# Folding the feature map into the projection weights: phi as the moving side, in two halves of the array

## The chip, the cores and the metric

The kernel runs on one core of a Trainium2 chip. The metric is the device time of one execution in microseconds (us), the median of the runs. A core has five engines that run side by side, each through its own list of instructions in order: TensorE (PE, with its weight loads shown apart as PEld), VectorE (DVE), ScalarE (ACT), GpSimd (POOL) and SyncE (SP), which here issues almost every DMA.

## The reference, cut to what matters

Two linear-attention blocks A and B of the same shape work on the same input and are mixed by a gate. Shapes: 2048 tokens, width 448, 16 heads of 28.

```
qkv   = x @ wqkv                      # per block: q, k, v, each 2048 x 448
pq,pk = q @ w_phi, k @ w_phi          # per head, 28 x 28
phi   = concat(softmax(p), softmax(-p))
kv    = phi_k^T v ;  z = sum phi_k    # per head
o     = phi_q kv / (phi_q z + 1e-6)
out   = g * (o_A @ wo_A) + (1 - g) * (o_B @ wo_B),   g = sigmoid(x . gate_w)
```

Softmax doesn't change when a constant is taken from all 28 features of a head. So phi may be folded into the weights, `x @ (wqkv_k @ w_phi)`, and the 28th feature subtracted from the others: 27 columns per head are left, 432 per block.

## The kernel before, in words

**Precision and tiles.** Every large product runs in fp32r (an fp32 of fewer mantissa bits) with both operands split into a high and a low part. A projection of one tile of 128 tokens for one block is 11 matmuls into one PSUM bank: 4 chunks of 128 rows high by high, 4 high by low, 3 low by high. The 2048 tokens are 16 tiles; two tiles share one load of x (512 KB, 256 tokens), called x0, x1, x2 and so on below. Each load is split by ACT (high) and DVE or POOL (low) into `rx`.

**Stages.** First the weights: `wv` (values, with the gate's column) is loaded and split; `wkt` and `wqt` (keys and queries, transposed, 448 rows of 512 columns per block) are loaded raw, multiplied by phi on the PE (the **fold**, four of them: K and Q for blocks A and B) and split into `rk` and `rq`. Then for each tile: values (V: banks `VA` and `VB`, one per block), keys (K: bank `K`), queries (Q: bank `Q`), softmax parts on ACT, DVE and POOL, and `kv_acc`, which adds phi_k by v into `T0`. At the end, from about 246 us, numerator, division, gate and output product.

**The fold before** (`load_wp`, `load_wt`, `fold`). The raw weights of one block stand in four groups of 28 partitions (one head each at partition 0, 32, 64, 96), loaded by four DMAs of 224 KB. The stationary side is `wpd`, phi less its 28th column, 28 x 32; the moving side is 128 columns of raw weights. That is 64 matmuls in fp32 per fold, on 16 tiles of 32 x 32 of the array, into a tensor `F` of four PSUM banks. The result has features in partitions, so DVE transposes all of `F` in one instruction (128 x 2048) into `ft` in SBUF; after that, four times, ACT copies a chunk to the high part and DVE (for two chunks of each Q fold POOL) subtracts to get the low part. `F` is one key: the next fold's matmuls wait until the transpose has read all of it.

**What sets the order.** All work is entered into a `Plan` by `add(engine, cost, ..., reads, writes)` in the order of `steps()`. PE keeps that order (`order` chains the PE steps). For the other engines and for SP a list scheduler picks, by the costs written in the code, the ready step with the earliest due time; SP steps also go through a model of the DMA queue, `moved = max(moved, t + 0.8) + kb / 360`, with the `kb` given to `add`. The list that comes out is fixed: on the chip every engine takes its instructions in that order and waits where one isn't ready. In `load_wt` the `kb` entered was 460 for a DMA of 224 KB. SP keeps eight DMAs in flight: a ninth waits for the first to land.

**Buffers.** `wkt` lies in `rt` slots 1 and 2. `wqt` lies in `re`, where the raw `wv` lay before, so it waits until `wv` is split. `ft` lies in `rt` slot 0 and in `ru`.

## Time and profile before

| What | Value |
|---|---|
| runs | 349.86, 349.91, 350.72 us; median 349.91 |
| profiled execution | 348.77 us, span of its instructions 347.0 us |
| granted TensorE clock | 0.998 of full |
| PE busy | 331.9 us (96% of the span) |
| DVE, POOL, ACT busy | 282.9 us (82%), 241.0 (69%), 145.8 (42%) |
| first key projection starts | 44.41 us |
| first query projection starts | 55.54 us in the chain of waits |
| numerator stage starts | 245.8 us |

The page's slices give each engine's busy share over time; the chain of waits follows the work that ended last back to its start; the table of windows gives busy time per stage, with the rate at which DMAs moved data. A matmul in fp32 leaves two records of a weight load and two of a matmul, so 64 matmuls are "x128".

### The profile page before, as it was taken

Reading aid. Unit: us, or ns where it says so; the run is one execution under the profiler, and the core shown is the slowest. Engines: PE = TensorE matmul, PEld = TensorE weight load, DVE = VectorE, ACT = ScalarE, POOL = GpSimd, SP = SyncE. Lnnn points to the kernel's source line nnn. Section 1 sums busy time; section 2 is a strip of 40 time slices with the busy share of each in tenths; the row PEclk is TensorE's granted clock in tenths of the full one; section 3 lists DMA queues with packets and bytes.
Section 4 is the critical chain, followed back from the end, with each engine's and each line's share of the span. In section 5 each row is a group of like instructions: output and inputs, shape, how many; then the busy total and the mean of one; then the engine's idle time right before and its main releaser. Section 6 shows DMA issues by size and latency. Waiting matters only on the chain.

```text
span 347.0 us, 9268 instructions
## 1 busy us (share of the span) xinstructions
PE 331.9 (96%) x3976; PEld 297.9 (86%) x3976; DVE 282.9 (82%) x342; ACT 145.8 (42%) x219; POOL 241.0 (69%) x195
## 2 busy tenths in 40 slices
PE   6985999999999999999999999999999999999995
PEld 5764799999999999999999999999888887787895
DVE  3647687897988979879898899987599999989780
ACT  3525684446426436345344543243043333443231
POOL 3003077999999988996987987795087769777600
PEclk9999999999999999999999999999999999999999
DMA  7998620641267497366536323377875545231111
GB/s 247 219 203 185 184 74 3 202 135 44 58 243 255 140 291 254 117 201 264 158 64 288 108 55 105 90 238 267 281 256 176 188 176 204 64 138 42 43 53 53
DMA packets 29488, 55.21 MB, mean 159 GB/s; under 512 B 4304, under 2 KB 23248, under 8 KB 27144
## 3 DMA queue, kind: packets, MB, share of 16 engines
q1 hardware_dynamic: 29320, 54.52, 50.1%
q8 instruction: 31, 0.51, 0.6%
q0 software_dynamic: 128, 0.12, 0.1%
q14 instruction: 9, 0.07, 0.1%
HBM read 32.00 MB, written 24.22 MB: 162 GB/s over the span
## 4 chain that ended last, share of the span: by engine, by line
PE 70%; DVE 16%; DMA 5%; POOL 3%; ACT 2%; issue 2%; SPq 1%; POOLq 0%; DVEq 0%; ACTq 0%
PE K L380 20%; PE Q L380 19%; PE VA L380 9%; PE VB L380 8%; PE O L597 8%; DVE rv L560 4%; PE T L467 4%; DMA re<-in_xt 3%; POOL rt L266 2%; DMA re<-in_wv 2%; DVE rt L512 2%; DVE T L585 2%; PE N L549 2%; DVE qsm L507 1%; DVE rx L266 1%
## 5 line engine op out<-in xcount | busy, mean ns | idle before, releaser
L380 PE MATMUL K<-rk,rx 128*128 128x432 f32 x352 | 72.2, 360 | 0.0
L380 PE MATMUL Q<-rq,rx 128*128 128x432 f32 x352 | 72.0, 359 | 0.0
L597 PE MATMUL O<-rk,rx 128*128 128x448 f32 x336 | 70.4, 368 | 1.5 <-ACT rx L269 1.5
L597 PEld LDWEIGHTS O<-rk,rx 128*128 128x128 f32 x336 | 62.5, 188 | 9.8 <-ACT rx L269 3.0
L380 PEld LDWEIGHTS Q<-rq,rx 128*128 128x128 f32 x352 | 66.0, 188 | 3.5 <-DVE ru L266 0.4
L380 PEld LDWEIGHTS K<-rk,rx 128*128 128x128 f32 x352 | 65.8, 188 | 3.5 <-issue 0.2
L266 POOL TENSOR_TENSOR re<-re,sm 128x896 f32<-128x896 f32 x32 | 54.0, 1709 | 6.2 <-DVE sm L456 5.2
L269 ACT ACTIVATE re<-re 128x896 f32<-128x896 f32 x32 | 30.5, 953 | 31.7 <-POOL re L266 31.7
L266 POOL TENSOR_TENSOR rt<-qmn,ru 128x896 f32<-128x896 f32 x16 | 28.3, 1766 | 16.9 <-DVE rt L512 10.9
L380 PE MATMUL VA<-rv,rx 128*128 128x450 f32 x154 | 34.7, 371 | 5.3 <-issue 3.6
L455 DVE TENSOR_REDUCE sm<-re 128x32 f32<-128x896 f32 x32 | 33.8, 1072 | 4.4 <-ACT re L269 4.4
L507 DVE TENSOR_REDUCE qsm<-rt 128x32 f32<-128x896 f32 x32 | 34.0, 1067 | 3.7 <-ACT rt L269 3.6
L380 PEld LDWEIGHTS VA<-rv,rx 128*128 128x128 f32 x154 | 28.5, 189 | 8.6 <-issue 4.0
L380 PE MATMUL VB<-rv,rx 128*128 128x448 f32 x154 | 33.5, 365 | 0.0
L269 ACT ACTIVATE rt<-ru 128x896 f32<-128x896 f32 x16 | 15.2, 953 | 40.3 <-issue 11.7
L380 PEld LDWEIGHTS VB<-rv,rx 128*128 128x128 f32 x154 | 28.9, 188 | 2.3
L512 DVE STREAM_TRANSPOSE rt<-rt 128x2048 f32<-128x2048 f32 x13 | 29.6, 2277 | 0.8 <-POOL rt L266 0.8
L266 POOL TENSOR_TENSOR re<-pk,mx 128x896 f32<-128x896 f32 x16 | 28.0, 1749 | 2.5 <-DVE mx L448 2.5
L266 POOL TENSOR_TENSOR rt<-rt,qsm 128x896 f32<-128x896 f32 x16 | 27.3, 1706 | 1.0
L266 POOL TENSOR_TENSOR re<-mx,pk 128x896 f32<-128x896 f32 x16 | 27.3, 1708 | 0.0
L269 ACT ACTIVATE pk<-K 128x896 f32<-128x896 f32 x16 | 14.8, 923 | 27.9 <-PE K L380 27.9
L569 POOL TENSOR_TENSOR rv<-rv,rd 128x896 f32<-128x896 f32 x14 | 23.8, 1703 | 1.1
(94 smaller groups left out, 460.5 us busy)
## 6 DMA issues: line engine op xcount, KB each, us to landing
ed<-rt SPq DMA_DIRECT2D x8, 1024.0 KB
qd<-ru SPq DMA_DIRECT2D x64, 112.0 KB
ru<-qd SPq DMA_DIRECT2D x16, 448.0 KB
re<-ed SPq DMA_DIRECT2D x5, 1024.0 KB
xraw<-in_xt SPq DMA_DIRECT2D x7, 512.0 KB
out<-re SPq DMA_DIRECT2D x16, 224.0 KB
wod<-wst SPq DMA_DIRECT2D x14, 224.0 KB
rk<-wod SPq DMA_DIRECT2D x2, 1568.0 KB
```

The lines of the kernel that those rows point to most:

```text
L266: return lambda: ENG[eng].tensor_tensor(val(o), val(a), val(b), op)
L269: return lambda: A.activation(val(o), val(i), f, **k)
L380: nc.tensor.matmul(bank[name][:, k, lo:hi], x[:, xc, o:o + P], w[l][:, c], start=i == 0, stop=i == len(XT) - 1)
L455: put("DVE", 2 * D, lambda s=s, e3=e3: V.tensor_reduce(sm[:, s], e3, AX.X, OP.add), [ke[s]], [("sm", t % 2, s)])
L467: nc.tensor.matmul(kvp()[32 * r:32 * r + DH + 1, b, g], vs[t % NV][:, b, h // 2, h % 2], es[t % NE][:, :, hs:hs + DH], start=(t == 0 and b ...
L507: put("DVE", 2 * D, lambda s=s, e3=e3: V.tensor_reduce(qsm[:, s], e3, AX.X, OP.add), [ke[s]], [("qsm", i, s)])
L512: add("DVE", 2.25, lambda: V.transpose(eTf[slot], eq.rearrange("p s a c f -> p (s a c f)")), ke, turned(slot))
L549: nc.tensor.matmul(bank["N"][32 * g:32 * g + 32, r, 2 * b * P:2 * b * P + 2 * P], kvt[32 * r:32 * r + 32, b, s, g], eTp[slots[0] // 2][32 ...
L560: add("DVE", 0.07 + 1.08 * nt, lambda: V.transpose(ctr().rearrange("p (r n) -> p r n", r=4), bank["N"][:, :, :2 * nt * P]), ["N"], [("ctr" ...
L569: put(eng, 2 * D, lambda: ENG[eng].tensor_tensor(mid["o", n % 3].rearrange("p (c a f) -> p a c f", c=4, a=8), ctv()[:, :, i, :, :DH], rd[: ...
L585: put("DVE", 4 * P + 50, lambda: V.transpose(ps().rearrange("p k (c t) -> p k c t", c=4), o()[:, :MID]), [("o", n % 3)], [kb])
L597: nc.tensor.matmul(bank[pb][:, 0, :D], a, w, start=i == 0, stop=i == len(terms) - 1)
```

## The change

The fold is turned round. The raw weights stand in two groups of 56 partitions (two heads each, at partition 0 and 64), loaded by two DMAs of 448 KB instead of four of 224. They become the stationary side: 56 x 128. The moving side is `bd`, a block-diagonal phi of 56 x 54: 27 features by two heads, zero where row and head don't belong together, made on DVE from phi and a mask that is loaded too. A fold is 32 matmuls (fp32, two halves of the array in turn), in two steps `jj` of 16, and its result has model rows in partitions and features in columns, which is the order that the projections want. The transposes and `ft` are gone: ACT and DVE read `F` in PSUM. All low parts are DVE's; POOL has none. `F` has four keys instead of one, so each step of a fold waits only for the readers of its two banks. `rk` and `rq` change their order to `b f h`, which a projection still reads as 432 columns in a row.

The buffers move as well: `wqt` goes to `rt` slot 0 and to `ru`, and no longer waits for `wv` to be split; `wpd` and `bd` lie in `ru`; `wv`'s raw rows keep `re` until the first K step. In `steps()` K 0 now stands ahead of V 4 and of the last fold. The planner's costs are new: 2.4 per fold (`FOLD`), and `kb = 917 // NB` = 458 for a DMA of 448 KB.

```diff
-    yield from (... ("FK", 0), ("x1",), ("V", 2), ("FK", 1), ("wq", 0), ("wq", 1), ("V", 3), ("x", 2))
-    yield from (("FQ", 0), ("V", 4, 0), ("FQ", 1), ("later",), ("K", 0), ("V", 4, 1), ("K", 1), ("wo_rows",))
+    yield from (... ("FK", 0), ("x1",), ("V", 2), ("FK", 1), ("wq", 0), ("wq", 1), ("V", 3), ("x", 2), ("FQ", 0), ("K", 0), ("V", 4, 0), ("FQ", 1), ("later",), ("V", 4, 1), ("K", 1), ("wo_rows",), ...
...
     def load_wt(k, b):
-        for q in range(4):
-            o, i = wts[k][b][32 * q:32 * q + DH], {"K": wkt, "Q": wqt}[k][b].rearrange("(g q d) c -> q d g c", q=4, d=DH)[q]
-            add("SP", 0.4, dma(o, i), [], [("wt", k, b, q)], lat=2, kb=460, ...)
+        for i in range(NB):
+            o = wts[k][b][64 * i:64 * i + PG]
+            r = {"K": wkt, "Q": wqt}[k][b].rearrange("(g p) c -> p g c", p=4 * DH)[PG * i:PG * i + PG]
+            add("SP", 0.4, dma(o, r), [], [("wt", k, b, i)], lat=2, kb=917 // NB, ...)
 
-    def fold(k, b, wh, wl, key, low):
...
-                        nc.tensor.matmul(bank["F"][32 * o:32 * o + 32, q, g * P:(g + 1) * P], wpd[32 * q:32 * q + DH, b, g],
-                                         wts[k][b][32 * q:32 * q + DH, g].rearrange("p (j o i) -> p o j i", o=4, i=32)[:, o], ...)
-        add("PE", 1.95, mm, [("wpd",), *[("wt", k, b, q) for q in range(4)]], ["F"])
-        add("DVE", 2.25, lambda: V.transpose(ft[b]..., bank["F"]...), ["F"], [ftk[b]])
-        for j in range(4):
-            add("ACT", 0.75, act(h, s), [ftk[b]], [(key, "h", j, b)])
-            add(e, {"DVE": 0.85, "POOL": 1.35}[e], tt(e, l, s, h.bitcast(F32), OP.subtract), ...)
+    def fold(k, b, wh, wl, key):
+        for jj in range(2):
+            def mm(jj=jj):
+                for m in range(2):
+                    for g in range(4):
+                        for i in range(2):
+                            j = 2 * jj + m
+                            nc.tensor.matmul(bank["F"][:, 2 * i + jj, :FW].rearrange("p (m f g q) -> p m g f q", ...)[:, m, g],
+                                             wts[k][b][64 * i:64 * i + PG, g, j * P:j * P + P], bd[64 * i:64 * i + PG, b, g], ...)
+            add("PE", FOLD / 2, mm, keys, [("F", 2 * i + jj) for i in range(2)])
+        for jj in range(2):
+            for i in range(2):
+                put("ACT", D, act(h, s), [("F", 2 * i + jj)], [key_h])
+                put("DVE", D + 50, tt("DVE", l, s, h.bitcast(F32), OP.subtract), [("F", 2 * i + jj), key_h], [key_l])
```

The scheduler's list moves at three places.

SP, the loads between `wv` and the third load of x. `in_xt` is x (x1 goes to `re`, the others to `xraw`), `in_wkt` and `in_wqt` are the raw weights. Before:

```order
L272 DMA rt<-in_wkt 28x4x512 x4
L272 DMA re<-in_xt 128x4x256
L272 DMA rt<-in_wkt 28x4x512 x4
L272 DMA xraw<-in_xt 128x4x256
L272 DMA re<-in_wqt 28x4x512 x8
L272 DMA xraw<-in_xt 128x4x256
```

and with the change:

```order
L273 DMA rt<-in_wkt 56x4x512 x2
L273 DMA re<-in_xt 128x4x256
L273 DMA rt<-in_wkt 56x4x512 x2
L273 DMA rt<-in_wqt 56x4x512 x2
L273 DMA ru<-in_wqt 56x4x512
L273 DMA xraw<-in_xt 128x4x256
L273 DMA ru<-in_wqt 56x4x512
```

The load of x2 (the first to `xraw` here) stood ahead of all of `wqt`; it now stands behind three quarters of it.

ACT, around the split of x2 (`rx<-xraw`); `vs_73` is the value tile 2, `vs_74` tile 3. Before:

```order
L269 ACTIVATE rx<-re 128x4x128 x2
L269 ACTIVATE vs_73<-VA 128x16x28
L269 ACTIVATE glog<-VA 128x1
L269 ACTIVATE rk<-rt 128x4x4x27 x3
L269 ACTIVATE vs_73<-VB 128x16x28
L269 ACTIVATE rx<-xraw 128x1024
L269 ACTIVATE rk<-rt 128x4x4x27
```

and with the change:

```order
L270 ACTIVATE rk<-F 128x216x2 x4
L270 ACTIVATE vs_73<-VA 128x16x28
L270 ACTIVATE glog<-VA 128x1
L270 ACTIVATE rx<-xraw 128x1024
L270 ACTIVATE vs_73<-VB 128x16x28
L270 ACTIVATE rk<-F 128x216x2 x4
```

The split of x2 stood behind the copy that empties bank `VB` of tile 2; it now stands ahead of it, and ahead of all four copies of the second K fold.

PE, from the first fold to the second key projection (`VA`, `VB` are one tile's values, `F` a fold). Before:

```order
L334 MATMUL F<-rt,wpd 32x128 x64
L380 MATMUL VA<-rv,rx 128x450 x11
L380 MATMUL VB<-rv,rx 128x448 x11
L334 MATMUL F<-re,wpd 32x128 x64
L380 MATMUL VA<-rv,rx 128x450 x11
L334 MATMUL F<-re,wpd 32x128 x64
L380 MATMUL K<-rk,rx 128x432 x22
L380 MATMUL VB<-rv,rx 128x448 x11
```

and with the change:

```order
L390 MATMUL VA<-rv,rx 128x450 x11
L390 MATMUL VB<-rv,rx 128x448 x11
L346 MATMUL F<-ru,rt 128x27x2 x32
L390 MATMUL K<-rk,rx 128x432 x22
L390 MATMUL VA<-rv,rx 128x450 x11
L346 MATMUL F<-ru 128x27x2 x32
L390 MATMUL VB<-rv,rx 128x448 x11
```

Both pieces begin in the third tile's values or just ahead of them; a key projection has moved ahead of the last fold, and all that follows stands as it did.

## The prediction, made before the changed kernel was run

> **What bounds the kernel now.** First the page's head, then the table of windows, cut where the chain of waits changes its kind.

> ```profile
> span 347.0 us, 9268 instructions
> PE 331.9 (96%) x3976; PEld 297.9 (86%) x3976; DVE 282.9 (82%) x342; ACT 145.8 (42%) x219; POOL 241.0 (69%) x195
> ...
> core 0: us, PE busy (x) PEld busy (x) DVE busy (x) ACT busy (x) POOL busy (x), PEclk, DMA share, GB/s
> 0.00:18.80 18.80, 14.88 (x71) 12.21 (x71) 7.96 (x18) 8.04 (x15) 3.35 (x14) 1.00 0.89 230
> 18.80:44.40 25.60, 19.65 (x568) 16.42 (x567) 15.83 (x15) 13.49 (x23) 3.93 (x5) 1.00 0.79 191
> 55.50:245.80 190.30, 190.09 (x1908) 177.68 (x1906) 165.56 (x200) 83.70 (x115) 165.13 (x114) 1.00 0.52 169
> ```

> From 55.5 to 245.8 us the PE is idle for 190.30 - 190.09 = 0.21 us in all. There the projections are the bound; work taken from DVE or POOL gains nothing, and a head that ends later or earlier moves the end by as much. The folds lie in 18.8 to 44.4, where the PE stands idle for 25.60 - 19.65 = 5.95 us. So the question is when the first query projection starts, now at 55.54. The chain of waits (start, length, what) and the chain's rows of the steady stage that I use as prices:

> ```profile
> 9.83 11.86 DMA re<-in_xt
> ...
> 22.39 2.52 PE VA L380 x11
> 24.90 2.22 PE VB L380 x11
> 27.12 2.04 PE F L334 x99
> 29.16 1.02 PE VA L380 x4
> 30.18 3.60 issue
> 33.78 1.60 PE VA L380 x7
> ...
> 44.48 4.52 PE K L380 x22
> 49.00 2.23 PE VB L380 x11
> 51.23 4.32 PE K L380 x22
> 55.54 4.32 PE Q L380 x22
> ...
> 88.30 1.71 PE T L467 x128
> 90.00 2.45 PE VA L380 x11
> ...
> 103.33 2.25 PE VA L380 x11
> ```

> The head is paced by loads. x1 lands at 21.7 and only then V 2 starts (22.39); a fold takes about 2 (2.04 here). The PE's idle time is 1.7 us ahead of V 2 (a fold ran from 18.77 to 20.67, its row stands further down), 3.6 us of "issue" in V 3 (it waits for no semaphore) and the rest mostly for the transpose ahead of the last fold.

> **The change, part by part.** First, one fold on the PE. It was 64 matmuls of 28 x 32 by 128 columns; it becomes 32 of 56 x 128 by 54 columns, each still as two passes, so 64 weight loads of 128 columns. No row shows this form; these are nearest:

> ```profile
> L334 PEld LDWEIGHTS F<-rt,wpd 28*32 28x32 f32 x256 | 3.2, 102 | 0.8 <-issue 0.6
> L380 PEld LDWEIGHTS K<-rk,rx 128*128 128x128 f32 x66 | 12.3, 188 | 0.8 <-issue 0.2
> L606 PEld LDWEIGHTS VB<-zero x5: 192/192/192, 4.8 to 5.3; 128*128 128x128 f32 x5
> L334 PEld LDWEIGHTS F<-rt,wpd x33: 101/104/105, 18.8 to 18.9; 28*32 28x32 f32 x33
> ```

> A load of 32 columns takes 102 ns, of 128 columns 188 ns: 86 ns for 96 columns, 0.90 ns a column, so 128 columns stream for about 0.115 us (the rest is latency). The fp32 matmuls of the warm-up follow each other at (5.3 - 4.8) / 4, about 0.12 us, so a load isn't longer. The matmul's own stream is short: kv's T row is 64 matmuls of 56 columns on four column strips in 1.71 us, 26.7 ns each, so two at a time 53 ns, 32 x 53 = 1.7 us.

> Do the two halves load side by side? The last row is a look at a fold's first 0.16 us (to 18.93): 33 loads of 32 columns begin there, 33 x 32 x 0.90 = 0.95 us of streaming. That is about five at a time, more than the four column strips of that fold, so groups of rows load side by side too. Then 32 x 0.115 = 3.7 us would be a fold's length; I take **3.6**, as the load may overlap a little better. The bounds: 1.7 if loads hide, 64 x 0.115 = 7.4 if one load goes at a time. I stay near the loads because two passes of 54 columns can't cover loads of 128.

> [...]

> Second, what x2's split waits for. Sizes and rates:

> ```profile
> xraw<-in_xt SPq DMA_DIRECT2D x7, 512.0 KB
> rt<-in_wkt SPq DMA_DIRECT2D x8, 224.0 KB
> re<-in_wqt SPq DMA_DIRECT2D x8, 224.0 KB
> ...
> 16.00:21.70 5.70, 4.67 (x143) 3.83 (x141) 0.00 (x0) 1.09 (x2) 0.00 (x0) 1.00 1.01 207
> 21.70:26.00 4.30, 3.61 (x18) 3.35 (x19) 3.56 (x5) 1.76 (x4) 0.00 (x0) 1.00 0.95 214
> 26.00:29.10 3.10, 3.10 (x135) 2.42 (x133) 2.08 (x4) 2.70 (x4) 0.00 (x0) 1.00 0.93 194
> ```

> The DMA engines are full (0.93 to 1.01) at 194 to 214 GB/s, so the order in SP's queue sets the landings. Before, behind x1 come half of `wkt` (896 KB) and x2 (512): 1.44 MB, 7.0 us at 205, landing 28.7. Now 896 + 896 + 448 + 512 KB stand there, 2.82 MB, 13.7 us: **35.4**. At 230 GB/s (the first window's rate) it is 34.0, at 191 36.4. Bytes, and 2 KB rows in HBM, stay as they were; I give 56 partitions no other rate.

> ACT and PE around it:

> ```profile
> 18.77 1.90 PE L334 MATMUL F<-rt,wpd 28*32 28x128 f32 x128
> ...
> 21.70 1.15 ACT L269 ACTIVATE rx<-re 128x512 fp32r<-128x512 f32 x2 [2.28 <-DMA re<-in_xt]
> 28.65 0.60 ACT L269 ACTIVATE vs<-VB 128x448 f32<-128x448 f32 x1
> 29.13 1.07 ACT L269 ACTIVATE rx<-xraw 128x1024 fp32r<-128x1024 f32 x1
> ...
> 35.21 2.38 PE L380 MATMUL VB<-rv,rx 128*128 128x448 f32 x11
> ...
> L269 ACT ACTIVATE rk<-ru 128x432 fp32r<-128x432 f32 x4 | 3.2, 968 | 0.0
> ```

> In the changed list ACT has x1's split done at 22.85, then a value copy, the four copies of the first K fold (0.6 like a value copy to 0.97 like now) and tile 2's VA, done by 26 to 28. There it stands at `rx<-xraw` until 35.4. Queued behind it are tile 2's copy out of `VB`, for which the PE's V 3 waits with its second half, and the second K fold's four copies, for which K 0 and the next fold wait. Split 1.07 and copy 0.60 give 37.1, so V 3's `VB` starts at **37.2**, not at 35.2 as now.

> The sum on the PE. First K fold 18.77 + 3.6 = 22.37: in the wait for x1, free. V 2 to 27.12 as now. Second K fold to 30.7 (its banks are read by then: ACT 23.4 + 4 x 0.97, DVE a copy later, 28.2). V 3's VA to 33.2 (2.45 behind a fold). Idle to 37.2, 4.0 us. Then VB 2.23, Q fold 3.6, K 0 4.52, V 4's VA 2.25, last fold 3.6, VB 2.43 (0.2 more behind a fold, as K 0 shows), K 1 4.32: 37.2 + 22.95 = 60.15. Against 55.54 that is **+4.6 us**. The 3.6 us of "issue" are gone, or lie in the hold: a fold leaves half as many instructions. If FK 1's readers hold the Q fold, up to 0.7 more (four copies from 37.2 at 0.97, low parts behind).

> Free on other engines: the DVE operations on phi and the mask (216 elements, now 0.38 each) fall in DVE's gap of 6.6 us ahead of x1's split; without that gap 1.3 us. Four transposes of 2.31 on DVE and four low parts on POOL are gone, DVE gets all 16 low parts; neither engine bounds what follows. SP and POOL issue fewer DMAs or as many.

> ```profile
> 15.40 0.38 DVE L266 TENSOR_TENSOR wpd<-wp 128x216 f32<-128x216 f32 x1
> ...
> 22.37 1.77 DVE L266 TENSOR_TENSOR rx<-re,rx 64x128 fp32r<-64x128 f32 x4 [6.59 <-ACT rx L269]
> 24.05 2.31 DVE L338 STREAM_TRANSPOSE rt<-F 128x2048 f32<-128x2048 f32 x1
> ```

> **The rivals.** One: the halves don't load side by side, 7.4 us a fold. For: no row has just two row strips. Against: the 33 loads. K folds end at 26.2 and 38.3, VA at 40.8, the hold vanishes, and 40.8 + 22.95 + 2 x 3.8 = 71.35: +15.8, 365.7 us.

> Two, on the other side: x2 isn't late. If its rows pass those of `wqt` in the DMA engines or `wqt` comes faster, VB starts at 33.2 and Q 0 at 56.15: +0.6, 350.5, no change. It decides from a landing at 31.4 down. For: each of 16 engines has its own work. Against: x1 took 11.86 us behind 1.6 MB, as a queue in order does. With a cheap fold on top it is 345.

> Three: loads hide and a fold takes 1.7, x2 late all the same: 37.2 + 22.95 - 3.8 = 56.35, +0.8, 350.7. For: T's rows run at their matmuls' pace. Against: those load 29 columns, these 128. At 2.4 a fold it is +2.2.

> The hold itself is an idle stretch of 4.0 us. The row at 33.78 shows what follows one of 3.6: seven matmuls in 1.60 us, 0.23 each against 2.25 / 11 = 0.20 in the steady stage, so I add nothing. [...] The trace doesn't bear that out at 3.6, and I give it 0.05 inside the forecast's share.

> **How the numbers follow.** The sum stands against the profiled execution, 348.77 us (span 347.0 and 1.8 around it); the median of the runs is 349.91, 1.1 above, and I add to that: 349.9 + 4.6 = **354.5 us**. Chances: forecast, folds of 2.7 to 5 us and x2 late, 0.54; rival one, wholly or in part, 0.13; two 0.13 (half of it faster); three 0.15 (half within 0.3%); something unseen 0.05. A measurement here can tell about 0.3%, 1.05 us. Faster: 0.065 of rival two, the unseen, and a few hundredths for folds cheaper than three says: 0.16. Same 0.14, slower 0.70. The range: the forecast alone, with folds of 2.7 to 5 and rates of 191 to 230, goes from 351.2 to 358.5; down to 349.5 it takes in rivals two and three, up to 359 some of rival one; outside lie most of one and the cheap corner of two.

> **What would show it.** In the changed profile: ACT idle ahead of `rx<-xraw` until about 35, released by a DMA; PE idle about 4 us ahead of tile 3's VB, released by ACT; a fold's busy time of about 3.6 (its weight loads filling it); no transposes; the first Q at about 60 with the PE full behind it. It is wrong if x2 is split before 32, if a fold takes under 2.5 or over 5, or if the PE gets new idle time after 60.

## The result: 354.3 us against 349.9, the forecast's total by other terms

The changed kernel takes 354.25 us (median of 4 runs, 353.44 to 355.12) and the kernel before 349.88 beside it (4 runs, 349.37 to 350.72): a ratio of 1.0123, with a 95% interval of 1.0092 to 1.0154. Forecast were 354.5 us. The first query projection starts at 60.36 us in the chain of waits, forecast 60.15. But of the terms that make up this number, two were wrong, in opposite directions.

The table of windows of the changed kernel, for the head cut where the granted clock changes (columns as before: stretch, its length, busy time of each engine, then PEclk, DMA share, GB/s), and for the steady stage:

```profile
core 0: us, PE busy (x) PEld busy (x) DVE busy (x) ACT busy (x) POOL busy (x), PEclk, DMA share, GB/s
14.00:27.98 13.98, 13.98 (x161) 12.89 (x159) 3.94 (x8) 4.49 (x10) 0.00 (x0) 1.00 0.96 238
27.98:31.39 3.41, 3.41 (x13) 2.96 (x12) 0.00 (x0) 0.94 (x1) 0.00 (x0) 0.50 0.52 110
31.39:38.22 6.83, 5.12 (x51) 4.36 (x50) 2.25 (x4) 3.34 (x9) 3.10 (x4) 1.00 0.36 107
38.22:45.05 6.83, 6.83 (x42) 6.46 (x41) 1.42 (x3) 2.00 (x4) 0.31 (x1) 0.50 0.60 180
45.05:60.36 15.31, 15.31 (x122) 14.34 (x122) 8.11 (x14) 5.61 (x10) 4.32 (x3) 1.00 0.11 28
...
60.00:250.00 190.00, 189.33 (x1901) 176.98 (x1900) 162.23 (x197) 81.57 (x114) 164.09 (x113) 1.00 0.50 163
```

From 60 us on the PE is nearly as full as it was (0.67 us idle in 190.00, against 0.21 in 190.30). In the head there are 1.71 us of idle time (6.83 - 5.12) where there were 5.95, and yet it ends later. The column to look at is PEclk: for 3.41 and 6.83 us the PE works at half its clock, with its busy time at 100% of the stretch. That costs half of 10.24 us, 5.1 us. The first profile of the kernel before has none of this; PEclk is 1.00 in its windows from 0 to 60 us.

PE's timeline of the changed kernel (start, length, engine, line, out<-in, count, and in brackets the idle time ahead and its releaser), and two rows of ACT's:

```profile
24.40 3.84 PE L346 MATMUL F<-ru,rt 56*128 56x54 f32 x64
28.17 3.98 PE L390 MATMUL VA<-rv,rx 128*128 128x450 f32 x11
32.00 2.50 PE L390 MATMUL VB<-rv,rx 128*128 128x448 f32 x11
36.21 5.28 PE L346 MATMUL F<-ru,rt 56*128 56x54 f32 x64 [1.71 <-DVE rk L267]
41.42 6.23 PE L390 MATMUL K<-rk,rx 128*128 128x432 f32 x22
```

```profile
17.18 1.15 ACT L270 ACTIVATE rx<-re 128x512 fp32r<-128x512 f32 x2 [2.73 <-DMA re<-in_xt]
30.45 1.06 ACT L270 ACTIVATE rx<-xraw 128x1024 fp32r<-128x1024 f32 x1 [6.95 <-DMA xraw<-in_xt]
```

A fold lasts 28.17 - 24.40 = 3.77 us, forecast 3.6. V 3's `VA` takes 3.98 us instead of 2.45, the Q fold 5.28 and K 0 6.23 instead of 4.6: these three lie in the half clock, wholly or in part. x1's split is at 17.18 us, forecast 21.7; x2's at 30.45, forecast 35.4. From one to the other it is 13.27 us, forecast 13.7. ACT does stand for x2, for 6.95 us, but the PE's idle time is 1.71 us ahead of the Q fold, not 4.0 ahead of tile 3's `VB`.

The balance at the first Q, from the rows of the two profiles: V 2 starts 2.65 us earlier (19.74 against 22.39); three folds behind it last 11.1 instead of 5.8 us, +5.3; half clock, +5.1; idle time of the PE behind V 2 1.71 instead of 3.60 + 0.64, -2.5. Together +5.3, measured +4.8 (60.36 - 55.54); the rest is in the overlap of starts and ends. (The rows of PE's timeline, which give the first Q of the kernels below, start a little earlier than the chain's: 60.20 here, 55.38 for the kernel before.)

On the chips of the experiments the kernel before itself ran from 344.4 to 352.7 us, and the printed ratios leave out the runs of either kernel that lie more than 1.5% above its fastest, so medians over all runs stand beside them.

### The profile page after: what moved, and what is told of

It is laid out like the page before. It is cut to its first block, busy times and chain, and to the rows that moved or that the text cites. A ratio compares the mean times of both kernels' runs of the same rounds, so it can differ in the third digit from the quotient of the medians.

```text
span 352.5 us, 8749 instructions
## 1 busy us (share of the span) xinstructions
PE 343.0 (97%) x3720; PEld 310.2 (88%) x3720; DVE 271.0 (77%) x346; ACT 139.1 (39%) x219; POOL 234.4 (67%) x192
## 4 chain that ended last, share of the span: by engine, by line
DVE 31%; PE 28%; DMA 17%; POOL 14%; issue 5%; ACT 4%; SPq 1%; POOLq 0%; DVEq 0%; ACTq 0%
PE O L607 7%; DVE rt L522 5%; PE K L390 5%; DMA ru<-qd 5%; POOL rt L267 5%; PE Q L390 5%; DMA xraw<-in_xt 5%; POOL re L267 4%; DMA ed<-rt 4%; DVE rv L570 4%; DVE qsm L517 3%; DVE sm L465 3%; POOL rx L267 3%; PE F L346 3%; DVE ru L267 2%
## 5 line engine op out<-in xcount | busy, mean ns | idle before, releaser
L390 PE MATMUL K<-rk,rx 128*128 128x432 f32 x352 | 73.8, 365 | 0.0
L390 PEld LDWEIGHTS K<-rk,rx 128*128 128x128 f32 x352 | 67.3, 192 | 3.5
L267 POOL TENSOR_TENSOR rt<-qmn,ru 128x896 f32<-128x896 f32 x16 | 28.2, 1766 | 17.5 <-DVE rt L522 10.6
L390 PE MATMUL VA<-rv,rx 128*128 128x450 f32 x154 | 35.9, 383 | 0.0
L267 POOL TENSOR_TENSOR rx<-xraw,rx 64x256 fp32r<-64x256 f32 (+1 forms) x12 | 15.5, 1295 | 27.4 <-ACT rx L270 26.5
L390 PEld LDWEIGHTS VA<-rv,rx 128*128 128x128 f32 x154 | 29.8, 197 | 2.8
L511 DVE TENSOR_REDUCE qmn<-ru 128x32 f32<-128x896 f32 x16 | 17.1, 1068 | 12.2 <-DMA ru<-qd 12.2
## 6 DMA issues: line engine op xcount, KB each, us to landing
xraw<-in_xt SPq DMA_DIRECT2D x7, 512.0 KB
out<-re SPq DMA_DIRECT2D x16, 224.0 KB
wod<-wst SPq DMA_DIRECT2D x14, 224.0 KB
```

Source lines behind the costliest of these rows:

```text
L267: return lambda: ENG[eng].tensor_tensor(val(o), val(a), val(b), op)
L390: nc.tensor.matmul(bank[name][:, k, lo:hi], x[:, xc, o:o + P], w[l][:, c], start=i == 0, stop=i == len(XT) - 1)
L511: put("DVE", 2 * D, lambda: V.tensor_reduce(qmn, tq.rearrange("p c b g f -> p c (b g) f"), AX.X, OP.min), [kt], [kn])
```

## Experiments: what halves the clock

The two halvings of the changed kernel last 3.41 and 6.83 us, and their starts lie 38.22 - 27.98 = 10.24 us apart: one, two and three times 3.41. Two theories were set against each other, both estimates from these numbers. Theory A: the granted clock follows the array's work in the stretch of 3.41 us before, and a fold's load-paced stream counts for so little that a stretch full of it passes for idle. Theory B: it is idle time, such as the 1.71 us.

**x2 early (e2_x2).** Only x2's load is moved: in the list of steps ahead of the query weights, which the planner then issues behind it.

```diff
-("FK", 1), ("wq", 0), ("wq", 1), ("V", 3), ("x", 2), ("FQ", 0),
+("FK", 1), ("x2",), ("wq", 0), ("wq", 1), ("V", 3), ("x", 2), ("FQ", 0),
...
+        elif what == "x2":
+            load_x(2)
```

> x2's load stands ahead of the whole of the query weights in SP's queue; nothing else is changed. x2 should then land at about 24 us instead of 30.4 (1.34 MB less ahead of it at about 216 GB/s), ACT no longer stands at rx<-xraw, and the 1.7 us of idle time ahead of the Q fold go: -1.7 us in any theory, if the readers of the second K fold are then done before V 3 is. The theories part over the TensorE clock. Theory A (a stretch of some 3.4 us that holds nothing but a fold's load-paced stream makes the clock gate halve the clock): both halvings stay, first Q at 58.7 us, 352.6 us. Theory B (the second halving comes from the 1.7 us of idle time): the second halving goes, and with it 3.4 us, first Q at 55.3, 349.2 us.

PE's timeline of this kernel, and the rows of its table of windows with half the clock:

```profile
25.99 3.78 PE L346 MATMUL F<-ru,rt 56*128 56x54 f32 x64
29.70 4.07 PE L390 MATMUL VA<-rv,rx 128*128 128x450 f32 x11
33.61 2.39 PE L390 MATMUL VB<-rv,rx 128*128 128x448 f32 x11
35.93 3.78 PE L346 MATMUL F<-ru,rt 56*128 56x54 f32 x64
39.64 4.59 PE L390 MATMUL K<-rk,rx 128*128 128x432 f32 x22
...
19.76:23.17 3.41, 3.41 (x11) 3.04 (x10) 1.19 (x3) 2.08 (x5) 0.00 (x0) 0.50 0.95 256
30.00:33.41 3.41, 3.41 (x11) 3.00 (x10) 1.51 (x3) 1.80 (x4) 0.40 (x2) 0.50 0.88 282
50.48:53.89 3.41, 3.41 (x11) 3.03 (x10) 2.54 (x4) 3.04 (x6) 0.00 (x0) 0.50 0.01 2
```

There is no idle time in this head, and the clock is halved three times all the same, from 19.76, 30.00 and 50.48 us, each time for 3.41 us. So theory B falls as the only cause. The starts lie 10.24 and 20.48 us apart, three and six times 3.41. If the head is cut into stretches of 3.41 us from there, the folds that are followed by a halving are those that fill one or nearly so: counted back from the halvings, the stretch that ends at 30.00 holds 3.11 us of fold and 0.30 of projection, and the one that ends at 40.24 holds 2.81 us of fold and 0.60 of projection: K 0 behind it runs at the whole clock (1.00 from 33.41 to 50.48). In this kernel the boundary lies between 0.36 (the stretch to 50.48) and 0.60 us of projection in 3.41.

The time is 349.17 us (10 runs, 346.75 to 353.86; ratio 0.9998, 0.994 to 1.0057; median of all 19 runs of before 350.66), and its spread is the clock: the four runs with a mean granted clock of 0.999 to 1.000 took 346.75 to 347.85 us, those with 0.985 took 350.83 to 351.82. That the median is the time which theory B gave (349.2) is luck: it lies between runs with and without halvings, and the profiled run, 351.82 us with its first Q at 58.34, is what theory A gave (352.6 and 58.7).

**The folds' halves between half projections (e3_mixed; e4_both with x2 early as well).**

```diff
-("FK", 0), ("x1",), ("V", 2), ("FK", 1), ("wq", 0), ("wq", 1), ("V", 3), ("x", 2), ("FQ", 0), ("K", 0), ("V", 4, 0), ("FQ", 1),
+("FK", 0, 0), ("x1",), ("V", 2, 0), ("FK", 0, 1), ("V", 2, 1), ("FK", 1, 0), ("wq", 0), ("wq", 1), ("V", 3, 0), ("FK", 1, 1), ("V", 3, 1), ("x", 2), ("FQ", 0, 0), ("K", 0, 0), ("FQ", 0, 1), ("K", 0, 1), ("FQ", 1, 0), ("V", 4, 0), ("FQ", 1, 1),
```

> Only the order of PE's work in the head is changed: each fold is cut in its two halves of about 1.9 us, and a half projection of V or K of 2.2 us stands between one half and the next. The same weight loads, the same matmuls, the same DMA order. Theory A (a fold's stream over a whole stretch of 3.4 us halves the clock): no granted clock of 0.5 anywhere in the head, V 3's VA and K 0 take 2.3 and 4.5 us again; x2 still holds ACT until 30.4, so tile 3's VB starts at about 32.1; first Q at about 55.6 us, 349.5 us. Theory B (folds of this form draw the clock down whatever stands between them, or the gate has another cause, such as loads from HBM): some 5 us of half clock stay, 353 to 355 us.

> The two edits together: x2's load ahead of the query weights, and the folds' halves between half projections. Theory A: no half clock and no hold of ACT; PE full from about 18.8 us; first Q at about 55.0 us, against 55.5 before the change and 60.4 after it; 348.5 to 349.5 us. Theory B: half clock stays for some 5 us, 352 to 354 us.

PE's timeline of the first, at the places where it differs, and of the second a stretch of the table of windows and the row of the first Q:

```profile
20.49 4.08 PE L390 MATMUL VA<-rv,rx 128*128 128x450 f32 x11 [0.76 <-ACT rx L270]
...
35.39 1.99 PE L346 MATMUL F<-ru,rt 56*128 56x54 f32 x32 [2.11 <-DVE rk L267]
37.31 4.06 PE L390 MATMUL VB<-rv,rx 128*128 128x448 f32 x11
```

```profile
18.40:55.46 37.06, 37.06 (x337) 33.27 (x336) 15.29 (x27) 15.17 (x30) 9.79 (x9) 1.00 0.52 134
```

```profile
55.46 4.46 PE L390 MATMUL Q<-rq,rx 128*128 128x432 f32 x22
```

The first was a miss: 357.61 us (4 runs; ratio 1.0287, 1.0207 to 1.0367), its first Q at 62.81 us where 55.6 was expected, with two halvings, from 20.73 and 37.80 us, each for 3.41. Both lie where half a fold of 1.9 us stands beside idle time: the stretch to 20.73 holds 1.99 us of fold, 0.76 of idle time and 0.66 of projection. So theory A was too narrow: idle time and the fold add up in one stretch (in the one to 37.80 it is 1.92 of fold and 1.00 of idle time). That run also had its x1 later than most (19.81). The second has the same halves and no idle time. There the clock is whole for 37 us, the first Q at 55.46 (55.0 expected), and the time 350.02 us (10 runs, 348.82 to 351.2; ratio 1.0022, 0.9983 to 1.006), half a microsecond over the expected. From 55.46 to 245.46 us its PE is idle for 2.00 us, against 0.67 from 60 to 250 in the changed kernel; no run here shows why. What halved the clock in this head is thus in the arrangement, not in the fold's work.

**A wider moving side (e5_wide; three times over in e6_narrow3 and e7_wide3).** Of a half's 16 matmuls, 12 stream 108 columns of phi instead of 54, and the surplus is written over by the next matmul. Theory A1: what counts is how much the array streams; the clock then stays whole, and the 5.1 us of half clock go from the 354.3, which leaves 349.2.

```diff
-                    for g in range(4):
+                    for g in (3, 2, 1, 0):
...
-... q=2)[:, m, g], wts[k][b][64 * i:64 * i + PG, g, j * P:j * P + P],
-                                             bd[64 * i:64 * i + PG, b, g], start=True, stop=True)
+                            lo = max(g - 1, 0)
+... q=2)[:, m, :, lo:g + 1], wts[k][b][64 * i:64 * i + PG, g, j * P:j * P + P],
+                                             bd[64 * i:64 * i + PG, b, lo:g + 1].rearrange("p g f q -> p f g q"), start=True, stop=True)
```

> The order of all work is that of the changed kernel. Only a fold's moving side is wider: 12 of 16 matmuls of a half stream 108 columns instead of 54 (the second 54 columns are written over by the next matmul, so the result is the same). The weight loads, their number and their pace stay: a fold of 3.7 to 3.9 us. [...] Theory A2 (the gate counts the load-paced stream, or half arrays, as idle whatever the columns): the half clock stays, 354.3 us.

PE's timeline of this kernel, and its one stretch of half clock from the table of windows:

```profile
24.49 3.78 PE L347 MATMUL F<-ru,rt 56*128 56x108 f32 x64
28.20 2.51 PE L391 MATMUL VA<-rv,rx 128*128 128x450 f32 x11
32.29 2.49 PE L391 MATMUL VB<-rv,rx 128*128 128x448 f32 x11 [1.58 <-ACT vs L270]
36.51 6.11 PE L347 MATMUL F<-ru,rt 56*128 56x108 f32 x64 [1.72 <-DVE rk L267]
...
37.61:44.44 6.83, 6.83 (x53) 6.61 (x52) 0.76 (x2) 1.00 (x2) 0.31 (x1) 0.50 0.61 180
```

The wide fold is no longer: 28.20 - 24.49 = 3.71 us, as the changed kernel's first (19.74 - 16.03), 0.116 for each of its 32 pairs of loads, so the columns hide behind the loads. On what halves the clock this run told nothing: at the whole clock none of its folds filled a stretch, and the one halving (from 37.61) followed one with 1.72 us of idle time. It did tell something on what brings the clock back. The halving lasted two stretches, and the first of them, 37.61 to 41.02, lies wholly within the wide fold: at a clock of 0.50 (this fold takes 6.11 us instead of 3.71) 108 columns didn't bring the whole clock back. Neither theory's time came (349.2 and 354.3): the median, 355.93 us, is no better than the changed kernel's, and the runs ranged from 350.32 (granted clock 1.000) to 357.63 (0.980); ratio 1.0129, 0.9935 to 1.0324. It shows something else, though: with `VA` at the whole clock, ACT's hold does reach tile 3's `VB` (1.58 us), and the Q fold on top (1.72).

To be free of where the stretches fall, the next two do the second K fold three times over.

```diff
-                for m in range(2):
+                for m in list(range(2)) * (3 if (k, b) == ("K", 1) else 1):
```

> The changed kernel with the matmuls of the second K fold done three times over (the same result, 11.1 us at the whole clock instead of 3.7), so that at least one whole stretch of 3.41 us of the clock gate lies within it wherever its grid falls. It starts at about 24.4 us. Theory A, in both its forms: the granted clock falls to 0.5 from 27.8 to 31.2 us on and stays so until a stretch behind the fold's end; the fold takes some 13 to 15 us. If the clock stays whole, theory A falls.

> The same with the wide moving side: 12 of 16 matmuls stream 108 columns instead of 54 behind the same weight loads, and the second K fold is done three times over. Theory A1 (the gate counts how much the array streams): the clock stays at 1.0 through a fold of 11.1 us. Theory A2 (it counts load-paced matmuls on half arrays as idle, whatever their columns): the clock falls to 0.5 as with the narrow one, and the fold takes 13 us or more.

The windows within that fold and its row of PE's timeline, first narrow, then wide:

```profile
26.11:30.26 4.15, 4.15 (x75) 4.15 (x76) 0.00 (x0) 0.00 (x0) 0.00 (x0) 1.00 0.94 201
30.26:43.02 12.76, 12.76 (x122) 12.66 (x121) 0.00 (x0) 1.49 (x2) 2.53 (x2) 0.50 0.42 125
...
26.11 16.98 PE L346 MATMUL F<-ru,rt 56*128 56x54 f32 x192
```

```profile
27.21:38.07 10.86, 10.86 (x193) 10.80 (x193) 0.00 (x0) 1.49 (x2) 2.53 (x2) 1.00 0.46 123
...
27.21 10.93 PE L347 MATMUL F<-ru,rt 56*128 56x108 f32 x192
```

Same weight loads, same number of matmuls, the same place: with 54 columns the clock falls to 0.50 4.15 us into the fold and stays there to its end; with 108 it stays at 1.00, and the fold takes 10.93 us instead of 16.98 (13 to 15 were expected for the narrow one). (The kernels took 364.22 and 357.44 us in one run each.) That is theory A1: what counts is how much the array streams, and PE's busy time, full in both, doesn't tell it. It is one run each, but both folds are long enough for at least two whole stretches of 3.41 us wherever these fall, and e8_wide_x2 below bears it out over 12 runs.

The halvings here are one, two or (e6_narrow3, 30.26 to 47.32 us) five times 3.41 us long, and the first of them starts at another place in each run (27.98 us in the changed kernel, 19.76 in e2_x2, 20.73 in e3_mixed, 37.61 in e5_wide). The profile can show the PE 100% busy ahead of one: it is 4.15 of 4.15 us above.

## Experiments: the loads, and the stall that went

**Each weight load of 56 partitions cut in two of 28 (e1_28rows).**

```diff
-            add("SP", 0.4, dma(o, r), [], [("wt", k, b, i)], ...)
+            def two(o=o, r=r):
+                for h in range(2):
+                    nc.sync.dma_start(o[DH * h:DH * h + DH], r[DH * h:DH * h + DH])
+            add("SP", 0.4, two, [], [("wt", k, b, i)], ...)
```

> The changed kernel with each weight load of 56 partitions cut in two of 28 partitions, one behind the other in the same queue; bytes, rows and order are the same. Theory L1 (56 partitions in one DMA are what makes the loads faster): back to some 205 GB/s behind the value weights, x1's split at 20 to 22 us, x2's at 34 to 35, first Q some 4 us later than in the changed kernel. Theory L2 (they make no difference): x1's split at 17 to 18 us, x2's at 30 to 31, as in the changed kernel.

ACT's timeline of this kernel:

```profile
21.04 1.15 ACT L270 ACTIVATE rx<-re 128x512 fp32r<-128x512 f32 x2 [5.62 <-DMA re<-in_xt]
36.78 1.06 ACT L270 ACTIVATE rx<-xraw 128x1024 fp32r<-128x1024 f32 x1 [8.19 <-DMA xraw<-in_xt]
```

x2's split, forecast at 35.4, is at 36.78 here; in the six profiles with whole loads and the same queue order it lies between 30.45 and 31.81. From x1's split to x2's it is 15.74 us here; in the five of those six in which both waited for their DMA it is 12.0 to 13.4. One run took 359.24 us, its first Q at 66.56 us, 6.4 behind the changed kernel's where some 4 were expected; its head has half clock too (V 2's `VA` takes 4.43 us, K 0 6.41), so this time gives no price of the loads. With hold and half clock out of the way the same was tried again on the last kernel below (e9_wide_x2_28, beside e8_wide_x2):

> The same as the kernel with the wide moving side and the early x2, but each weight load of 56 partitions cut in two of 28. With neither hold nor half clock in the way, what differs is the loads alone. Theory L1 (one DMA to 56 partitions is faster than two to 28): x1's split at 20 to 21 us instead of 17 to 18, first Q about 3 us later, 349 to 351 us. Theory L2 (no difference but from run to run): the same within 1 us.

ACT's timeline, whole loads (e8_wide_x2), then cut ones (e9_wide_x2_28):

```profile
17.01 1.15 ACT L270 ACTIVATE rx<-re 128x512 fp32r<-128x512 f32 x2 [2.36 <-DMA re<-in_xt]
23.59 1.06 ACT L270 ACTIVATE rx<-xraw 128x1024 fp32r<-128x1024 f32 x1 [0.37 <-DMA xraw<-in_xt]
```

```profile
20.30 1.15 ACT L270 ACTIVATE rx<-re 128x512 fp32r<-128x512 f32 x2 [4.87 <-DMA re<-in_xt]
27.38 1.06 ACT L270 ACTIVATE rx<-xraw 128x1024 fp32r<-128x1024 f32 x1 [2.43 <-DMA xraw<-in_xt]
```

The cut loads bring x1 3.3 and x2 3.8 us later, and the kernel takes 348.67 us instead of 347.61 (12 runs each; ratios 1.0081, 1.0037 to 1.0125, and 1.0037, 1.0000 to 1.0074): 1.1 of the 3 us expected. In both V 2 follows the end of the first fold and does not wait for x1, and that fold, which waits for its weights with the cut loads, ends 1.7 us later (V 2 at 21.68 against 19.94, first Q at 55.58 against 53.83). The runs of the two overlap (346.64 to 350.94 against 346.52 to 348.83), and each landing is that of one profile. Whether the partitions, the number of DMAs or the bytes under way matter is left open.

**The kernel before again (b_again), and with its second K fold in halves (b_halves).**

> The kernel before, once more, for how much its landings vary from run to run. Theory L1 (the loads of the changed kernel are faster because each reaches 56 partitions with one DMA): x1's split starts at 21 to 22 us here as in the first profile. Theory L2 (the 4.5 us between the two kernels are variation from run to run): anything from 17 to 22. The stall of 3.6 us in V 3 that waits for nothing should come again, and no granted clock of 0.5.

PE's timeline of that profile and a stretch of its windows:

```profile
19.90 2.52 PE L380 MATMUL VA<-rv,rx 128*128 128x450 f32 x11 [1.05 <-ACT rx L269]
22.25 2.38 PE L380 MATMUL VB<-rv,rx 128*128 128x448 f32 x11
24.57 0.41 PE L334 MATMUL F<-rt,wpd 28*32 28x128 f32 x4
25.50 1.86 PE L334 MATMUL F<-rt,wpd 28*32 28x128 f32 x124 [0.53 <-issue]
27.29 1.09 PE L380 MATMUL VA<-rv,rx 128*128 128x450 f32 x4
33.62 2.78 PE L380 MATMUL VA<-rv,rx 128*128 128x450 f32 x7 [5.23 <-issue]
36.20 3.73 PE L380 MATMUL VB<-rv,rx 128*128 128x448 f32 x11
...
32.29:39.12 6.83, 5.50 (x15) 4.90 (x15) 1.20 (x2) 2.68 (x5) 0.00 (x0) 0.50 0.81 218
```

Of the expectations here, the whole clock was a miss, and so were the 21 to 22 us of theory L1. The stall of V 3 is 5.23 us long this time, and the clock is halved behind it for 6.83 us. So the kernel before has the half clock too: of 29 runs beside the last experiments, 2 had a mean granted clock of 0.999 or more (344.42 and 344.49 us), the others 0.980 to 0.998 (345.5 to 352.7). The first profile, with 3.60 us of stall, was one of its better runs. x1's split is at 19.22 us, against 21.70 in the first profile and 16.93 in the next one: 28-partition loads alone vary by 4.8 us from run to run and can be as early as whole ones, so the first two profiles exaggerate the gain in the loads. With whole 56-partition loads nine profiles give 16.92 to 19.81, 17.7 on the mean.

```diff
-("V", 2), ("FK", 1),
+("V", 2, 0), ("FK", 1, 0), ("V", 2, 1), ("FK", 1, 1),
...
-            for g in range(4):
+            for g in gs:
...
+        for gs in ((0, 1), (2, 3)) if part is None else (((0, 1), (2, 3))[part],):
+            add("PE", 1.95 / 2, lambda gs=gs: mm(gs), ...)
```

> The kernel before with its second K fold cut in two halves, one ahead of V 2's VB and one behind it; nothing else is changed. Theory F1 (the stall of 3.6 and 5.2 us in V 3, which waits for no semaphore, comes because a whole fold uses up 256 instructions in 1.9 us, faster than they are delivered): two halves with 2.2 us of projection between them leave less than 1.5 us of it; first Q 2 to 3.6 us earlier, 346.5 to 348 us. Theory F2 (it depends on something else, such as the place in the program or the loads at that time): the stall stays at 3 to 5 us, 350 us.

PE's timeline with the halves; then the instruction queue's row from the view of the DMA queues, first kernel before, 30 to 32 us (packets, MB, share of 16 engines):

```profile
17.61 2.50 PE L383 MATMUL VA<-rv,rx 128*128 128x450 f32 x11
21.64 0.45 PE L334 MATMUL F<-rt,wpd 28*32 28x128 f32 x15 [1.53 <-DVE rt L341]
24.26 1.09 PE L334 MATMUL F<-rt,wpd 28*32 28x128 f32 x49 [2.18 <-issue]
25.29 3.87 PE L383 MATMUL VB<-rv,rx 128*128 128x448 f32 x11
29.09 1.07 PE L334 MATMUL F<-rt,wpd 28*32 28x128 f32 x64
30.09 1.09 PE L383 MATMUL VA<-rv,rx 128*128 128x450 f32 x4
33.20 1.60 PE L383 MATMUL VA<-rv,rx 128*128 128x450 f32 x7 [2.02 <-issue]
```

```profile
q8 instruction: 1, 0.02, 3.9%
```

The stall isn't shortened, it is divided: 2.18 + 2.02 us. Between the two places lie 49 + 11 + 64 + 4 = 128 matmuls, 256 instructions with their loads; in the kernel before it is the same 124 + 4. The first of the two places stands, in both kernels, 26 matmuls behind the start of V 2 (11 + 11 + 4 in b_again, 11 + 15 here). Theory F1's cure failed, and theory F2's place in the program has its part. As an estimate from these counts, instructions come in pieces of 256 with bounds at fixed places of the program, 8.1 and 8.9 us from the end of one stall to that of the next (25.50 to 33.62, 24.26 to 33.20); two halves within the same two pieces then change nothing. A packet of the instruction queue shows ahead of the end of each of these stalls: between 31 and 32 us in the first profile of before (end at 33.78), 22 to 26 and 30 to 32 in b_again (25.50 and 33.62), 18 to 22 and 30 to 32 in b_halves (24.26 and 33.20). That fits, but no row names what the PE waits for, so how fast instructions are delivered isn't shown. The clock is halved here as well, from 24.91 to 28.32 us, behind the first stall. In the changed kernel 128 matmuls are 64 of a fold and 64 of projections, 3.7 + 64 x 0.2, about 16.5 us as an estimate, and the stall is in neither of its profiles. Why e7_wide3, with 192 fold matmuls in 10.93 us, shows none is open: the DMA engines are only 0.46 busy there, but no run separates the two. With two short stalls instead of a long one b_halves takes 348.78 us (12 runs; ratio 1.0067, 1.0021 to 1.0113; median of all 29 runs of before 350.78).

## The two cures together, and the changed kernel once more

The wide moving side and x2's early load, each as above, with the changed kernel's order on PE.

> Two edits on the changed kernel: the fold's wide moving side (108 columns in 12 of 16 matmuls), which keeps the clock whole if theory A1 is right, and x2's load ahead of the query weights, which takes ACT's hold away. The order on PE is that of the changed kernel. PE full from FK 0 on: x1's split at 17 to 18, first Q at 53.3 to 54.5 us (58.34 with the narrow fold and x2 early, less three halvings of 1.7 us each), no granted clock of 0.5 after the start; 346 to 348 us against 349.9 of the kernel before and 354.3 of the changed one. If the wide side is no cure, 349 to 353.

> The changed kernel once more, on the chip of the three others: for its landings, its half clock and its time beside theirs. Theory A: one to three stretches of half clock in the head, at other places than in its first profile as the grid of 3.41 us falls; 352 to 356 us.

Windows and the first Q of e8_wide_x2, then two rows of PE's timeline of after_again:

```profile
16.23:53.83 37.60, 37.60 (x368) 35.16 (x368) 15.72 (x28) 16.11 (x32) 7.56 (x8) 1.00 0.57 145
...
53.83 4.46 PE L391 MATMUL Q<-rq,rx 128*128 128x432 f32 x22
```

```profile
32.89 2.49 PE L390 MATMUL VB<-rv,rx 128*128 128x448 f32 x11 [0.95 <-ACT vs L270]
37.11 3.80 PE L346 MATMUL F<-ru,rt 56*128 56x54 f32 x64 [1.72 <-DVE rk L267]
```

PE is full at the whole clock from the first fold on, and the first Q starts at 53.83. The time is 347.61 us (12 runs, 346.52 to 348.83, granted clock 0.999 or more in each). The same kernel with the narrow fold, e2_x2 on another chip, had a clock below 0.999 in 6 of its 10 runs; this pair is the broadest evidence for theory A1. The changed kernel on the same chip took 354.94 (6 runs, 353.06 to 356.62; ratio 1.026, 1.0203 to 1.0316), so the two cures are worth 7.3 us. Against the kernel before it is 0.9% faster by the medians (350.78) and has little more than a quarter of its spread (2.3 against 8.3 us); against the fastest runs of before it isn't faster (1.0037). In after_again one halving (from 40.74 us, 3.41 long) follows the one fold that filled a stretch, and with `VA` at the whole clock the hold shows again in both places, 0.95 and 1.72 us.

## Why the prediction was right, and where it wasn't

- **A fold of 3.6 us**: right, 3.71, 0.116 us for a pair of loads. The halves load side by side, at 3.71 / 64 = 0.058 us for a load where the warm-up's follow each other at 0.12, and the loads set the length: twice the columns cost nothing (3.71 in e5_wide too). Rivals one and three fall with it. (The 33 loads of the prediction are 0.95 / 0.16, about six at a time and not five; nothing hangs on it.)
- **x1 at 21.7, x2 at 35.4**: wrong. The price behind x1 held: x2 comes 13.27 us after it, forecast 13.7 (2.82 MB at 205 GB/s). The step that failed is the start of this sum, x1 at 21.7, taken over from one profile of the kernel before; it came at 17.18, 4.5 us earlier. In part that is variation, since the 28-partition loads of before gave 16.93 to 21.70 in three profiles. In part it may be "I give 56 partitions no other rate": x1 is at 17.7 on the mean of nine profiles with whole loads and at 20.30 and 21.04 in the two with cut ones. How much is which isn't shown.
- **ACT's hold**: the mechanism was right (6.95 us at `rx<-xraw`, with `VB`'s copy and the second K fold's copies behind it), the size and place were not. The sum had 4.0 us ahead of tile 3's `VB` and at most 0.7 ahead of the Q fold; it is 0 to 1.58 and 1.71 to 1.72. In the first profile the half clock in `VA` hides the former.
- **"So I add nothing" for the clock**: wrong, and the largest miss, 5.1 us in the first profile. A half clock was weighed, at 0.05, for the hold alone, as idle time, and no window of the head of the kernel before showed one (PEclk 1.00); that a load-paced fold at full busy time could bring it, alone (e6_narrow3, 0.50 from 4.15 us into the fold) or with idle time (e3_mixed, 1.99 + 0.76 us), was in no step. The row that I judged by (3.60 us of stall without a halving) was one run's luck: behind 5.23 us in b_again the clock was at 0.50 for 6.83 us.
- **The stall of 3.6 us in V 3 gone**: right. The 256 instructions from one stall to the next in b_again and b_halves fit the reason given, that a fold leaves half as many (64 matmuls with their loads for 128); that the stall comes back with more of them in the changed kernel wasn't tried.
- **From the first Q on nothing changes**: right, 189.33 of 190.00 us busy.
- **Rival two (x2 not late, no change)**: its condition, a landing by 31.4, was met in the first profile. Its price of 350.5 was missed for the clock; e8_wide_x2, without hold and half clock, is at 347.6.

The sum of 60.15 us became 60.36 because -2.65 (V 2 early) and -2.3 (a hold of 1.7 instead of 4.0) stand against +5.1 (half clock). That the two sides cancel is luck. The time was right; as a chain of causes the prediction was half right.

## What to carry to other kernels

A PE that the profile shows 100% busy can run at half the clock: where loads of 128 columns pace matmuls with a short moving side (54 columns here), look at the granted clock, and if it falls, put denser work between them (e4_both, 1.00 over 37.06 us) or stream more columns, which cost nothing here while the loads set the pace (108 columns, a fold of 3.71 us with either). The wider stream kept a whole clock here (e7_wide3, 1.00 over 10.86 us); it didn't bring a halved one back (e5_wide, 0.50 over 6.83 us). Cover idle time beside such work first, for in e3_mixed the two added up. And where a kernel's runs differ by per cents, read the mean clock of each run before a single profile is taken for the kernel.
